# An attention and gated-projection kernel with its whole schedule rewritten, and 65 matmuls on a zero tile added to its opening

## The chip, the cores and the metric

One core of one Trainium2 chip runs the kernel. The metric is the device time of one execution in microseconds (us). The engines are PE (TensorE; PEld is its weight load), DVE (VectorE), ACT (ScalarE), POOL (GpSimd) and SP (SyncE, which here only issues transfers).

## The reference

The first part is causal attention over 4 batches, 8 heads, 768 positions and head size 64. Heads 0, 2 and 6 see all earlier positions, the others only 4 sink positions and a window of 64. The second part is a gated projection of the result.

```python
scores = scale * np.matmul(q, k.transpose(0, 1, 3, 2))
mask = np.where(retr[0, :, 0, 0, None, None], full_mask, stream_mask)
scores = np.where(mask[None, :, :, :], scores, -1000000000.0)
scores = scores - np.max(scores, axis=-1, keepdims=True)
a = np.exp(scores)
a = a / (np.sum(a, axis=-1, keepdims=True) + 1e-09)
attn = np.matmul(a, v)                    # (4, 8, 768, 64)
x = attn.transpose(0, 2, 1, 3).reshape(3072, 512)
h = x @ w_in                              # w_in: (512, 2048)
g = h * (1.0 / (1.0 + np.exp(-beta * h)))
out = g @ w_out                           # w_out: (2048, 512)
```

## The kernel before

The work is cut into 8 chunks (a batch and a half of its 768 positions, 384 rows each) and every chunk into 4 units (a pair of heads), 32 units in all. For a unit, keys and queries are cast to bf16 (`cast`, L246) and turned by PE (`transpose_qk`, L322; from chunk 3 on by transfers), copied to SBUF (`copy_qk`, L330 and L333), multiplied into scores (`steps_QK`, L451), put through the exponential on ACT (L460) and multiplied with the values (`steps_PV`, L520). A column of ones in the value tile gives the sum of a row, by which `normalize` (L529, L533) divides. A pair of units is turned into `xT` (`steps_X` L558 and `copy_x` L567, or by a transfer).

A chunk's rows then go through the first projection in 16 groups (`steps_G1`, L588, then tanh on ACT L593 and the gate on DVE L596) and through the second in blocks of four groups of weights (`steps_G2`, L641). Group i of the first projection needs block i//4 of `w_in`, and step i of the second needs block i of `w_out`; POOL loads these blocks (`load_w_in` L140, `load_w_out` L144). The second projection of chunk 0 is allowed when all its 16 groups are done.

For the first 8 units the masks are added on PE, as a matmul of a mask tile with the identity (`begin`, L422); later units multiply by masks on DVE. At the start, `idle(8, ...)` lets PE do eight matmuls on a tile of zeros (L167). Keys and queries of chunks 0 to 2 are loaded by SP (`load_qk`, L119) and values too (`load_v`, L132); with the letter `g` a load waits for a small fill of its tile on POOL (L115, L129).

The order on every engine is written out by hand. `RAMP` is a list of words that `do` carries out one after the other; each engine keeps the order in which the words give it work. A word has an operation, a unit or chunk, a part, and the engine (v: DVE, a: ACT, g: POOL):
- `ck`, `cq`: cast of keys or queries; `tk`, `tq`: their transposes; `kk`, `kq`: the copies out of PSUM; `ko`: copies for the sink positions
- `ad`: mask matmuls; `qk`: scores; `ex`: exponential; `ma`: a mask on DVE
- `cv`: cast of values; `vo`: sink values; `on`: fills with ones; `pv`: two of a unit's six value products; `no`: normalize
- `xx`, `cx`: transposes and copy to `xT`; `ne`: mask tiles; `be`: the gate's factors
- `lv`, `lq`: loads by SP; `wi`, `wo`: loads of weights by POOL; `ro`: row loads by POOL for chunk 3 and later (L282); `rq`, `rk`: their tiles
- `mm`, `mA`: one group of the first projection (for `mA` in a buffer of the scores); `mb`: one step of the second (four matmuls); `hm`, `hf`: the two halves of one group; `tt`: all transposes and copies of a unit.

`PLAN` has one line for each later unit: `V` scores, `p` a value product, `T` transposes, `X` transposes to `xT`, `a`, `A` and `b` projections, beside words as above. Score tiles have two buffers (`ps_s`), `ps_o` one, and the tiles named `mm` three.

Of the kernel before, what the change touches and what calls it, by code (L numbers as in the profile page):

```python
# [10 lines left out]
F32 = mybir.dt.float32  # L11
# [7 lines left out]
def kernel(  # L19
# [13 lines left out]
    nc = tc.nc  # L33
    B, H, S, D = q.shape
# [5 lines left out]
    HT = HALF // 128  # L40
# [20 lines left out]
    ps_o = ctx.enter_context(tc.tile_pool(name="ps_o", bufs=1, space=bass.MemoryType.PSUM))  # L61
# [94 lines left out]
    zeros = consts.tile([128, 512], BF16, name="zeros")  # L156
# [160 lines left out]
    def transpose_qk(u, name):  # L317

        s = st_u.setdefault(u, {})
        tp = ps_m.tile([128, 512], F32, name="mm").bitcast(BF16)[:, 0:HALF].rearrange("p (t j) -> p t j", t=HT)  # L320
        for t in range(HT):
            nc.tensor.transpose(tp[:, t, :], s["qkb"][:, "qk".index(name), t].rearrange("p h d -> p (h d)"), ident)  # L322
        s["t" + name] = tp
# [58 lines left out]
    def steps_QK(u):  # L382
# [117 lines left out]
        some = 3 if len(tiles) == 3 else 2  # L500
        return [visit(range(i, min(i + some, len(tiles)))) for i in range(0, len(tiles), some)]

    def steps_PV(u):
        b, h2, p = units[u]
        s = st_u.setdefault(u, {})

        def head(hh, qi, last):
            def go():
                for f in s["masks"] + chunk_values[u // NPAIR] if u >= 8 else []:
                    f()  # L510
                if "po" not in s:
                    if u < 8 and u % 2:
                        po = ps_m.tile([128, 512], F32, name="mm")
                        s["po"] = po[:, 0:HT * 2 * (D + 1)].rearrange("p (t h d) -> p t h d", t=HT, h=2)
                    else:
                        s["po"] = ps_o.tile([128, HT, 2, D + 1], F32, name="po")
                po = s["po"]
                lst = s["blocks"][hh][qi]
                for j, (e, val) in enumerate(lst):
                    nc.tensor.matmul(po[:, qi, hh, :], e, val, start=(j == 0), stop=(j == len(lst) - 1))  # L520
                if last and u >= 8:
                    normalize(u)
            return (len(s["blocks"][hh][qi]) * 38, go)
        return [head(hh, qi, hh == 1 and qi == HT - 1) for qi in range(HT) for hh in range(2)]
# [138 lines left out]
    h = FO // 2  # L663
# [21 lines left out]
    def do(word):  # L685

        what, n, i, eng = re.fullmatch(r"([a-z]{2}|[a-z][A-Z])(\d*)\.?(\d*)([vag]?)", word).groups()
        n, i = int(n or 0), int(i or 0)
        if what in ("ck", "cq"):
            cast(n, what[1], copies[eng])  # L690
        elif what in ("tk", "tq"):
            step((170, lambda: transpose_qk(n, what[1])))
        elif what in ("kk", "kq"):
            copy_qk(n, what[1], copies[eng])
        elif what == "ko":
            sinks_of(n)
        elif what in ("ad", "qk", "ex", "ma"):
            if n not in visits:
                visits[n] = steps_QK(n)
            step((0 if what in ("ex", "ma") else 170, lambda: visits[n][what](i)))  # L700
        elif what == "cv":
            cast_v(n, i, copies[eng])
        elif what == "vo":
            sink_values(n)
        elif what == "pv":
            pv = products.setdefault(n, [])
            if not pv:
                pv.extend(steps_PV(n))
            run(pv[:2])
            del pv[:2]  # L710
        elif what == "no":
            normalize(n)
        elif what == "xd":
            x_by_dma(n)
        elif what == "xx":
            run(steps_X(n))
        elif what == "cx":
            copy_x(n, copies[eng])
        elif what == "on":
            ones_v(engines[eng], n)  # L720
        elif what == "ne":
            negatives([(0, 1, 2), (3, 4)][n])
        elif what == "be":
            step((100, beta_go))
        elif what == "lv":
            load_v(n, held=eng == "g", tiles=[i])
        elif what == "lq":
            load_qk(n, i, held=eng == "g")
        elif what == "wi":
            load_w_in(n)  # L730
        elif what == "wo":
            load_w_out(n)
        elif what == "rq":
            rows_queries()
        elif what == "rk":
            rows_keys()
        elif what == "ro":
            if n not in more_rows:
                more_rows[n] = load_rows(n)
            more_rows[n].pop(0)()  # L740
        elif what in ("dk", "dq"):
            transposes_dma(n, what[1])
        elif what == "ml":
            late[n].pop(0)()
        elif what == "tt":
            run(steps_T(n))
        elif what == "hm":
            opened.append(done[0])
            done[0] += 1
            step(halves[0](opened[-1], 0))  # L750
        elif what == "hf":
            step(halves[0](opened.pop(0), 1))
        else:
            feed({"mm": "a", "mA": "A", "mb": "b"}[what])

    def feed(x):
# [34 lines left out]
    PLAN = """
        ro3 ro3 ck9v b cq9a dk3 b cv2.1v cv2.0v vo2 T ro3 cv2.2v V cq11v a ro3 ro3 ro3 ck11a ro4 a b
        ck10a a dq3 a p cq10v a V p T p p p V p
        b T b p p p p p V p
        A b A a V ro4 p V a p p ro4 p p p
        ro4 V b p p p b p p ro4 p V b
        b p p p p X V p p a ro4 a ro4
        b A ro4 a a p V p ro4 p p ro4 b ro4 a a A ro4 A b b b dk4 A V a p dq4 p b A b
        p p p p p V p a a
        p p A p V p p p  # L800
        a a b b p p p p p p V a A A
        a b p p p p V p p
        b b a V p p p p p b a p
        b A A a a A p a A A a p b a p A p p p A A V b b b A
        p V p p p p p
        a A a b b p p p V p p b p a A
        a p A b p b p b A p b a p b p V A a
        V a p p b p p b V p p A
        b p p p p V p p
        A a b V b b a a p p b p A p a p a a A A p b V a b A b b  # L810
        p p p p V p p
        a A V b p A A p p p V p p a A
        a p b V b p p p p p
        V b a p a p p V A p A b b p p A A a
        p b V a p p p p A a p
        b a A p a p a a b a A p p A b a p b a p
        b A X a A b A
    """.strip().split("\n")
# [41 lines left out]
    i = 0  # L860
# [39 lines left out]
```

## Time and profile before

| | |
|---|---|
| median of 3 runs | 228.62 us (228.47 to 229.1) |
| the profiled execution | 231.07 us |
| its span, first to last instruction | 229.1 us |
| PE busy | 223.1 us, 1907 matmuls |
| ACT, DVE, POOL busy | 154.3, 141.8, 87.6 us |
| first projection starts | 24.41 us |
| second projection starts | 48.65 us |

A row of the timeline gives the start, the time from first start to last end, the engine, the line, the operation, the tiles (out<-in), the shape and the count, and in brackets the idle time before it and what ended that. A row of a stretch gives its length, then the busy time and the number of instructions of PE, PEld, DVE, ACT and POOL (of PE alone where only PE was asked for), the clock that the throttle granted, the mean share of the DMA engines (over 1 where packets overlap) and GB/s. A row of waits gives the engine, tile and line that waited, what it waited for, the sum in us, how often, and the longest. Matmuls of one row overlap, so a row is as long as the steps between them and one's own duration.

### The profile page before, as it was taken

How to read it: one execution, taken by the hardware profiler on the slowest of the kernel's cores; microseconds unless marked ns; L12 is line 12 of the kernel's file. 1: busy time of each engine (PE TensorE's matmuls, PEld its weight loads, DVE VectorE, ACT ScalarE, POOL GpSimd, SP SyncE). 2: the span in 40 equal slices, each digit the busy share in tenths (PEclk: the TensorE clock that was granted, in tenths of full speed). 3: DMA queues.
4: the chain of work that ended last, by engine and by line, in shares of the span. 5: the costliest groups of instructions: out<-in, count | busy, mean ns of one | idle time of the engine just before them, and what ended most of it. 6: DMA issues, size and time to landing. Idle time of an engine off the chain costs nothing.

```text
span 229.1 us, 5018 instructions
## 1 busy us (share of the span) xinstructions
PE 223.1 (97%) x1907; PEld 127.4 (56%) x1907; DVE 141.8 (62%) x342; ACT 154.3 (67%) x254; POOL 87.6 (38%) x143
## 2 busy tenths in 40 slices
PE   7899999999999999999999999999999999999994
PEld 2456666654565665555654565455654656455553
DVE  4458988875286588536952588546963779028600
ACT  2567988864868799438944697759876878138621
POOL 5373991219636269535028038940560000000000
PEclk9999999999999999999999999999999999999999
DMA  6999999999999999969778969496983130111012
GB/s 202 262 297 247 215 197 203 232 193 161 196 142 97 181 164 156 122 173 156 111 149 109 158 132 173 86 163 93 194 70 83 47 83 0 49 46 46 0 49 92
DMA packets 95383, 31.66 MB, mean 138 GB/s; under 512 B 81776, under 2 KB 92416, under 8 KB 95360
## 3 DMA queue, kind: packets, MB, share of 16 engines
q1 hardware_dynamic: 58880, 22.82, 48.6%
q0 software_dynamic: 35904, 8.13, 39.8%
q10 hardware_dynamic: 576, 0.40, 0.5%
q8 instruction: 15, 0.25, 0.4%
q14 instruction: 8, 0.07, 0.1%
HBM read 27.27 MB, written 6.29 MB: 146 GB/s over the span
## 4 chain that ended last, share of the span: by engine, by line
PE 94%; DMA 2%; ACT 1%; SPq 0%; issue 0%; ACTq 0%
PE mm L641 35%; PE mm L588 25%; PE sp L588 12%; PE sp L451 8%; PE po L520 7%; PE mm L322 2%; DMA s<-in_k_dram 2%; PE sp L422 2%; PE mm L626 2%; PE mm L558 1%; PE mm L520 1%; PE mm L451 1%; ACT qkb L246 1%; SPq L119 0%; ACT es L460 0%; ACT KT L330 0%
## 5 line engine op out<-in xcount | busy, mean ns | idle before, releaser
L641 PE MATMUL mm<-w_out_sb,gT 128*128 128x512 bf16 x368 | 85.9, 379 | 0.0
L460 ACT ACTIVATE es<-sp 128x768 bf16<-128x768 f32 (+2 forms) x72 | 56.6, 837 | 21.4 <-PE sp L451 21.2
L588 PE MATMUL mm<-xT,w_in_sb 128*128 128x384 bf16 x348 | 64.6, 326 | 0.0
L588 PEld LDWEIGHTS <-w_in_sb 128*128 128x128 bf16 x512 | 47.8, 98 | 29.8 <-issue 0.2
L593 ACT ACTIVATE th<-mm,beta_h 128x384 f32<-128x384 f32 x87 | 49.7, 587 | 5.7 <-PE mm L588 0.9
L641 PEld LDWEIGHTS <-gT 128*128 128x128 bf16 x368 | 33.4, 98 | 36.0 <-issue 1.5
L596 DVE SCALAR_TENSOR_TENSOR gT<-th,mm 128x384 bf16<-128x384 f32 x87 | 46.7, 551 | 6.7 <-ACT th L593 3.2
L282 POOL DMA_DIRECT2D s<-in_q_dram x30 | 22.4, 763 | 26.3 <-DMA QTD<-s 19.8
L588 PE MATMUL sp<-xT,w_in_sb 128*128 128x384 bf16 x164 | 32.3, 326 | 0.0
L645 ACT ACTIVATE osb<-mm 128x512 f32<-128x512 f32 x23 | 13.9, 603 | 25.5 <-PE mm L641 25.2
L520 PEld LDWEIGHTS <-es 128*128 128x128 bf16 x472 | 23.8, 99 | 12.8 <-issue 1.5
L596 DVE SCALAR_TENSOR_TENSOR gT<-th,sp 128x384 bf16<-128x384 f32 x41 | 22.3, 552 | 5.6 <-ACT th L593 3.7
L282 POOL DMA_DIRECT2D s<-in_k_dram x30 | 22.4, 760 | 8.5 <-DMA w_out_sb<-in_moe_w_out_dram 5.8
L593 ACT ACTIVATE th<-sp,beta_h 128x384 f32<-128x384 f32 x41 | 23.7, 585 | 2.3 <-PE sp L588 0.2
L520 PE MATMUL po<-VX,es 128*128 128x65 bf16 x360 | 25.2, 195 | 0.0
L251 POOL CAST VX<-vs 128x512 bf16<-128x512 f32 x16 | 10.1, 632 | 36.4 <-DMA vs<-in_v_dram 30.2
L529 DVE RECIPROCAL rec<-po 128x6 f32<-128x6 f32 x28 | 5.4, 193 | 29.1 <-PE po L520 29.1
L451 PE MATMUL sp<-QTD,KT 64*128 64x128 bf16 (+2 forms) x258 | 20.1, 249 | 0.6 <-ACT QTD L333 0.4
L478 DVE TENSOR_TENSOR es<-es,Mh 128x768 bf16<-128x768 bf16 (+1 forms) x26 | 15.5, 626 | 5.0 <-ACT es L460 4.4
L533 DVE TENSOR_TENSOR x<-po,rec 128x384 bf16<-128x384 f32 x28 | 15.6, 557 | 1.0
L451 PEld LDWEIGHTS <-KT 64*128 64x128 bf16 x278 | 11.4, 96 | 6.2 <-issue 3.9
L259 POOL COPY VO<-VX 128x512 bf16<-128x512 bf16 x16 | 10.8, 696 | 6.2 <-DVE VX L251 6.2
(72 smaller groups left out, 160.3 us busy)
## 6 DMA issues: line engine op xcount, KB each, us to landing
vs<-in_v_dram SPq DMA_DIRECT2D x24, 256.0 KB, 5.2
out_dram<-osb SPq DMA_DIRECT2D x23, 256.0 KB, 2.6
w_in_sb<-in_moe_w_in_dram POOLq DMA_DIRECT2D x4, 512.0 KB, 9.3
w_out_sb<-in_moe_w_out_dram POOLq DMA_DIRECT2D x4, 512.0 KB, 16.8
s<-in_k_dram POOLq DMA_DIRECT2D x30, 64.0 KB, 4.8
s<-in_q_dram POOLq DMA_DIRECT2D x30, 64.0 KB, 4.9
s<-in_k_dram SPq DMA_DIRECT2D x4, 384.0 KB, 6.8
s<-in_q_dram SPq DMA_DIRECT2D x4, 384.0 KB, 6.5
```

Of the source, the lines that this page charges most:

```text
L259: copy(out=vo[:, i - 1, :, 0:D], in_=vx[:, i, :, 0:D])
L282: nc.gpsimd.dma_start(out=ROWS[c % 2, name][:, t, i * 4 * D:(i + 1) * 4 * D].rearrange("p (h d) -> p h d", d=D), in_=src[b, i:H:2, r:r + 1 ...
L451: nc.tensor.matmul(sps[i][r][:, x * 128:y * 128], key(a, lhs), s["QT"][half(a), qi * 128:(qi + y - x) * 128], start=first, stop=first or y ...
L460: nc.scalar.activation(out=views[i].rearrange("p r k j -> p r (k j)"), in_=banks[2][:, :, 0:n * 128], func=ACTF.Exp, scale=scale)
L478: nc.vector.tensor_mul(ev[:, :, 0:n], ev[:, :, 0:n], Mh[h2][:, None, m0:m0 + n].to_broadcast([128, 2, n, 128]))
L520: nc.tensor.matmul(po[:, qi, hh, :], e, val, start=(j == 0), stop=(j == len(lst) - 1))
L533: nc.vector.tensor_mul(xg[g][:, :, :, u % 2, :].rearrange("p a t d -> p t a d"), po[:, :, :, 0:D], rec.to_broadcast([128, HT, 2, D]))
L588: nc.tensor.matmul(hp[:, 0:HALF], w_in_sb[:, mo, fi * 128:(fi + 1) * 128], xT[c][:, mo, :], start=(mo == 0), stop=(mo == MO - 1))
L593: nc.scalar.activation(out=th, in_=hp[:, 0:HALF], func=ACTF.Tanh, scale=beta_h[:, fi:fi + 1])
L596: nc.vector.scalar_tensor_tensor(out=gTs[c][:, fi, :], in0=th, scalar=1.0, in1=hp[:, 0:HALF], op0=ALU.add, op1=ALU.mult)
L641: nc.tensor.matmul(op, gTs[c][:, fi, ns * 128:(ns + 1) * 128], w_out_sb[:, fi, :], start=(fi == 0), stop=(fi == FO - 1))
L645: nc.scalar.activation(out=osb, in_=op, func=ACTF.Copy, scale=0.5)
```

## The change

Both lists are rewritten. The same operations stand in them in another order, some on another engine: for instance the casts `ck3`, `cq3`, `ck6`, `cq6` and `cq7` go to ACT, and `cv0.2` goes from ACT to DVE. The halves `hm` and `hf` become an ordinary group. `tt8` stands in front of all five `mb` of the opening instead of after two; of the six `ro3` in the opening one now stands in front of `wo3`.

A new word, `zz`, calls `keep_busy`: n matmuls of the zero tile with itself, each 122 columns wide, into the columns of the PSUM tile of unit 0's value product that the product does not use. Nobody reads them. The tile of the value product gets the full width of 512 columns for that. There are six lots of ten and one of five: in front of `tq0`, `tq1`, `ad0.0`, `ad0.1`, `ad1.0`, `qk1.0` and the second `pv0`.

```diff
+    banks_o = {}
+
+    def sums_bank(u):
+        if u not in banks_o:
+            banks_o[u] = ps_o.tile([128, 512], F32, name="po")
+        return banks_o[u]
+
+    def keep_busy(n):
+        z = HT * 2 * (D + 1)
+        for i in range(n):
+            nc.tensor.matmul(sums_bank(0)[:, z:512], zeros[:, 0:128], zeros[:, 0:512 - z], start=True, stop=True)
...
-                        s["po"] = ps_o.tile([128, HT, 2, D + 1], F32, name="po")
+                        s["po"] = sums_bank(u)[:, 0:HT * 2 * (D + 1)].rearrange("p (t h d) -> p t h d", t=HT, h=2)
...
     RAMP = """
-        ck0g ne1 lv0.0 lv0.1 tk0 ck2a ne0 cq0v ck1a tq0 kq0a ad0.0 on0v lv0.2 kk0v cq1v tq1 qk0.0
-        tk2 ad0.1 kq1v tk1 kk1v lq1.0g be qk0.1 ex0.0 ad1.0 cv0.0g ko1 lq1.1 ex0.1 pv0 ck3v cq3g tk3
-        lv1.0g cq2a tq2 kk3v lv1.1 cv0.1g ad1.1 qk1.1 kk2v ex1.1 tq3 ko2 qk1.0 wi0 vo0 cq4g lv1.2 cv0.2a
-        lq2.0g ko3 pv0 kq2v pv0 ad2.0 qk2.0 lv2.0 ex1.0 pv1 kq3a pv1 ck4v ad2.1 qk2.1 lv2.1 pv1 ex2.0
...
-        kk6a ml0 tk5 cq7g kq5v ex4.1 kk5a ko5 ko6 ad5.1 tq6 wi1 qk5.0 ex4.0 tk7 tq7 ex5.0 no3
...
-        pv7 pv7 no7 wo3 pv6 no6 rk cq8g xx2 ro3 cx2a mA mA ck8g xx3 cx3a mm mA
...
-        mA mm ro3 mA mm ro3 mm mm ro3 mA mA mb mb tt8 mb mb mb
+        ne1 ck1a on0g lv0.0g ck0g cq0v zz10 tq0 ck2a ne0 cq1v kq0a zz10 tq1 tk0 kk0v zz10 ad0.0 tk2 lv0.1 qk0.0 tk1
+        cq2v zz10 ad0.1 lv0.2 lq1.0g kk1v ck3a ex0.0 kq1a kk2v be qk0.1 zz10 ad1.0 ad1.1 ko1 tk3 lq1.1 cv0.0g tq2
+        ex0.1 cq3a lv1.0g ko2 tq3 pv0 lv1.1 kk3a ko3 wi0 qk1.1 cv0.1v zz10 qk1.0 kq2a vo0 ex1.1 ad2.0 kq3v qk2.0
+        cv0.2v lv1.2 zz5 pv0 ck4v pv0 lq2.0g ex2.0 ad2.1 qk2.1 no0 pv2 cq4g ex1.0 cq5g pv1 pv1 tk4 lv2.0 ad3.0 pv1 no1
+        qk3.0 ad3.1 qk3.1 ex2.1 pv2 tq4 ck6a xx0 kk4v pv2 ex3.0 tk6 kq4v ad4.0 cx0v pv3 ck7g ad4.1 pv3 ad5.0 tq5 ml0
+        on1g qk4.1 ex3.1 cq6a no2 kk6a ck5g pv3 cq7a lv2.1 qk4.0 tk5 tq6 ad5.1 ex4.1 kq5v kk5a ko5 ko6 qk5.0 tk7 tq7
+        lv2.2 no3 qk5.1 ex4.0 wi1 ex5.0 wi2 ex5.1 lq2.1 kq6v kq7v xx1 ad6.0 ml1 ml1 qk6.0 ma5.0 ad6.1 qk6.1 cx1a wi3
...
+        ex7.0 qk7.1 ex7.1 pv5 pv5 rk wo1 pv5 mm wo2 pv6 lv3.1 pv7 cq8g pv6 no5 pv6 pv7 ro3 pv7 no6 no7 wo3 xx2 cx2a
...
+        mm mA mm mA mm mA mb mb mb mb mb
     """
...
     PLAN = """
-        ro3 ro3 ck9v b cq9a dk3 b cv2.1v cv2.0v vo2 T ro3 cv2.2v V cq11v a ro3 ro3 ro3 ck11a ro4 a b
...
+        ck9v dk3 ro3 cq9v A ro3 cv2.0v T cv2.1v vo2 ro3 ro3 cv2.2v V ro3 a b ro3 cq11v
...
```

More of the change, by code (lines that the diff above doesn't have):

```diff
@@ L746, in do @@
             run(steps_T(n))
+        elif what == "zz":
+            keep_busy(n)
         elif what == "hm":
@@ L771 @@
     RAMP = """
-        ck0g ne1 lv0.0 lv0.1 tk0 ck2a ne0 cq0v ck1a tq0 kq0a ad0.0 on0v lv0.2 kk0v cq1v tq1 qk0.0
-        tk2 ad0.1 kq1v tk1 kk1v lq1.0g be qk0.1 ex0.0 ad1.0 cv0.0g ko1 lq1.1 ex0.1 pv0 ck3v cq3g tk3
-        lv1.0g cq2a tq2 kk3v lv1.1 cv0.1g ad1.1 qk1.1 kk2v ex1.1 tq3 ko2 qk1.0 wi0 vo0 cq4g lv1.2 cv0.2a
-        lq2.0g ko3 pv0 kq2v pv0 ad2.0 qk2.0 lv2.0 ex1.0 pv1 kq3a pv1 ck4v ad2.1 qk2.1 lv2.1 pv1 ex2.0
-        ad3.0 tq4 no0 tk4 ex2.1 ck7g kk4a qk3.0 ad3.1 qk3.1 no1 pv2 ck6v ex3.0 cq5v ck5g pv2 tk6
@@ L777 @@
-        xx0 ad4.0 cq6g pv3 kq4v ex3.1 pv2 ad4.1 cx0v ad5.0 qk4.1 pv3 lv2.2 no2 on1g tq5 pv3 qk4.0
-        kk6a ml0 tk5 cq7g kq5v ex4.1 kk5a ko5 ko6 ad5.1 tq6 wi1 qk5.0 ex4.0 tk7 tq7 ex5.0 no3
-        qk5.1 ex5.1 kq6v xx1 ad6.0 kk7v wi2 kq7v wi3 cx1a qk6.0 ml1 ad6.1 ex6.0 cv1.1g ko7 qk6.1 cv1.0v
-        ex6.1 hm lq2.1 ma5.0 ma5.1 mm cv1.2g vo1 mm wo0 pv4 lv3.0g ad7.0 lv3.1 pv4 hf pv4 no4
-        qk7.0 ad7.1 pv5 pv5 ex7.0 lv3.2 qk7.1 pv5 no5 ml1 wo1 ex7.1 pv6 pv6 wo2 mm pv7 rq
-        pv7 pv7 no7 wo3 pv6 no6 rk cq8g xx2 ro3 cx2a mA mA ck8g xx3 cx3a mm mA
@@ L783 @@
-        mm mA mm mm mA mm mm mm mA mm ro3 mm mm mA mm mm mm ro3
-        mA mm ro3 mA mm ro3 mm mm ro3 mA mA mb mb tt8 mb mb mb
+        ne1 ck1a on0g lv0.0g ck0g cq0v zz10 tq0 ck2a ne0 cq1v kq0a zz10 tq1 tk0 kk0v zz10 ad0.0 tk2 lv0.1 qk0.0 tk1
+        cq2v zz10 ad0.1 lv0.2 lq1.0g kk1v ck3a ex0.0 kq1a kk2v be qk0.1 zz10 ad1.0 ad1.1 ko1 tk3 lq1.1 cv0.0g tq2
+        ex0.1 cq3a lv1.0g ko2 tq3 pv0 lv1.1 kk3a ko3 wi0 qk1.1 cv0.1v zz10 qk1.0 kq2a vo0 ex1.1 ad2.0 kq3v qk2.0
+        cv0.2v lv1.2 zz5 pv0 ck4v pv0 lq2.0g ex2.0 ad2.1 qk2.1 no0 pv2 cq4g ex1.0 cq5g pv1 pv1 tk4 lv2.0 ad3.0 pv1 no1
@@ new lines @@
+        qk3.0 ad3.1 qk3.1 ex2.1 pv2 tq4 ck6a xx0 kk4v pv2 ex3.0 tk6 kq4v ad4.0 cx0v pv3 ck7g ad4.1 pv3 ad5.0 tq5 ml0
+        on1g qk4.1 ex3.1 cq6a no2 kk6a ck5g pv3 cq7a lv2.1 qk4.0 tk5 tq6 ad5.1 ex4.1 kq5v kk5a ko5 ko6 qk5.0 tk7 tq7
+        lv2.2 no3 qk5.1 ex4.0 wi1 ex5.0 wi2 ex5.1 lq2.1 kq6v kq7v xx1 ad6.0 ml1 ml1 qk6.0 ma5.0 ad6.1 qk6.1 cx1a wi3
+        ex6.0 ex6.1 ma5.1 cv1.1g kk7v mm cv1.0g ko7 mm cv1.2g vo1 lv3.0g rq ad7.0 mm pv4 pv4 pv4 ad7.1 qk7.0 wo0 no4
+        ex7.0 qk7.1 ex7.1 pv5 pv5 rk wo1 pv5 mm wo2 pv6 lv3.1 pv7 cq8g pv6 no5 pv6 pv7 ro3 pv7 no6 no7 wo3 xx2 cx2a
@@ L785 @@
+        lv3.2 mA mA mm ro3 xx3 cx3v mm mA mm ck8a mm mA mA mm ro3 ro3 mm mA mm mm mm mA mm mm mA mm tt8 ro3 mA mm ro3
+        mm mA mm mA mm mA mb mb mb mb mb
     """
@@ L791 @@
     PLAN = """
-        ro3 ro3 ck9v b cq9a dk3 b cv2.1v cv2.0v vo2 T ro3 cv2.2v V cq11v a ro3 ro3 ro3 ck11a ro4 a b
[L793 to L817, printed above, removed]
+        ck9v dk3 ro3 cq9v A ro3 cv2.0v T cv2.1v vo2 ro3 ro3 cv2.2v V ro3 a b ro3 cq11v
+        b b A dq3 A ro4 p p V ck11a p ck10a p p p b cq10v V b T
+        b T b p V p p p p p b a
+        a p p V p p V A p p
+        V a b p p V p p p p ro4 A
+        ro4 ro4 b X p V b p p b A p p p a ro4 b
+        ro4 a p V ro4 p p p a a ro4 ro4 b A ro4 A dk4 b a ro4 ro4 a p A V dq4 a p a b
+        p p p A p V p p
+        A b A p p p p p p A V
+        A a p p b p p V p a a p a
+        b p p V p p p p
+        b a a p V p p p p p a
+        a A A b b p a A A a p a a p b A p p b a V p A a A a
+        p V p a A p p p p
+        b A A a b p p p b p a a p p b V b a A
+        A p a a A a A a p V p p p p a a
+        p V p a b V p p p p A b
+        p p a p p V p p
+        b V b p b p a p V b p A p p b a A b A a A a
+        b b A p p b p p p a V p A b a
+        p V a A p p p A p V p b A
+        p p V p p p p
+        b V A a a V A p b p b a A A p p b a p p a
+        A b b p b V a p a A b p A p A p b a p a A
+        p p p p p p
+        A a X a A A A b b
     """.strip().split("\n")
```

## The prediction

> **What bounds the kernel now.** I read the page first, then PE's waits, then PE's busy time by stretch.
>
> ```profile
> PE 223.1 (97%) x1907; PEld 127.4 (56%) x1907; DVE 141.8 (62%) x342; ACT 154.3 (67%) x254; POOL 87.6 (38%) x143
> ...
> PEclk9999999999999999999999999999999999999999
> DMA  6999999999999999969778969496983130111012
> ...
> PE 94%; DMA 2%; ACT 1%; SPq 0%; issue 0%; ACTq 0%
> ```
> ```profile
> PE mm L167 <- DVE zeros L157: 1.3, 1, 1.3
> PE mm L322 <- DVE qkb L246: 0.7, 2, 0.5
> PE sp L451 <- ACT QTD L333: 0.4, 1, 0.4
> ```
> ```profile
> 24.40:225.00 200.60, 200.60 (x1699) 115.06 (x1696) 126.52 (x303) 139.43 (x229) 74.55 (x105) 1.00 0.89 125
> ```
> PE is 94% of the chain. From 24.4 us, where the first projection begins, it is busy in all 200.60 us of 200.60 (the second column), so the new order can gain nothing there; it can only open a gap. Whatever is won must be won before 24.4 us, and it stays won only if nothing later, above all a transfer, holds PE up. The DMA row is at 9 from the second slice to the seventeenth (5.7 to 97 us): transfers have no reserve in that time.
>
> In the ramp PE waits little (1.1 us besides the start), but it is slow. The PEclk row does not show that; the durations of equal rows on PE's timeline do:
>
> ```profile
> 1.29 3.59 PE L167 MATMUL mm<-zeros 128*128 128x512 bf16 x8 [1.29 <-DVE zeros L157]
> 4.83 0.50 PE L322 MATMUL mm<-idb,qkb 128*128 128x128 bf16 x3
> 5.51 0.50 PE L322 MATMUL mm<-idb,qkb 128*128 128x128 bf16 x3 [0.17 <-DVE qkb L246]
> ...
> 12.47 0.50 PE L322 MATMUL mm<-idb,qkb 128*128 128x128 bf16 x3
> ...
> 17.10 0.66 PE L322 MATMUL mm<-idb,qkb 128*128 128x128 bf16 x6
> ...
> 18.70 0.33 PE L322 MATMUL mm<-idb,qkb 128*128 128x128 bf16 x3
> ...
> 34.35 1.46 PE L588 MATMUL mm<-xT,w_in_sb 128*128 128x384 bf16 x8
> ```
> ```profile
> L167 PE MATMUL mm<-zeros 128*128 128x512 bf16 x8 | 3.6, 628 | 1.3 <-DVE zeros L157 1.3
> ...
> L588 PE MATMUL mm<-xT,w_in_sb 128*128 128x384 bf16 x348 | 64.6, 326 | 0.0
> ```
> Three transposes take 0.50 us at 4.83 and at 12.47, but 0.33 at 18.70. So PE runs slow until about 17.4 us, inside the row at 17.10 (six in 0.66). Matmuls of a row overlap, so their step is what is left of the row without one's own duration (the groups' means above): the zero matmuls step by (3.59 - 0.63)/7 = 0.42 us for 512 columns, 0.83 ns a column; the projections by (1.46 - 0.33)/7 = 0.16 us for 384, 0.42 ns a column. The ramp runs at half speed.
>
> **What brings full speed.** The ramp's slow part with all engines, and two stretches of it, PE alone:
>
> ```profile
> 4.83:17.43 12.60, 11.39 (x94) 6.43 (x94) 6.93 (x20) 7.12 (x12) 6.64 (x20) 1.00 1.18 281
> ```
> ```profile
> 10.61:14.02 3.41, 3.29 (x33) 1.00 1.08 315
> 14.02:17.43 3.41, 3.41 (x33) 1.00 1.21 273
> ```
> The switch came after a stretch without a gap that began between 10.61 and 14.02, so after 3.4 to 6.8 us. The unbroken stretch from 1.29 to 5.33 (the 0.17 us gap before 5.51) brought none, so 4.0 us were not enough there. In the new order the first ten zero matmuls stand behind the eight that exist, the first transposes have their data by then, and ten more follow; PE has no gap from 1.29 to about 7 us. I estimate the switch 4.0 to 6.8 us after 1.29, at 5.3 to 8.1, and take 6.5.
>
> [...]
>
> **The price of the zero matmuls.** Each has 512 - 390 = 122 columns: 0.10 us slow, 0.051 us fast. A lot of ten costs 1.0 or 0.51. The first lot and most of the second run slow (1.0 + 0.75), the other 45 fast (2.3): about 4.1 us of PE in all. PE's own work from 4.83 to 20.9 us (the transposes ahead of the key copy `kk5a`) halves in its slow part: the 11.39 us busy of the row above would be about 5.7, and 3.5 (17.4 to 20.9) follow. From 4.7, the end of the eight: 4.7 + 5.7 + 3.5 + 4.1 = 18.0, against 20.9 now. So PE stops setting the pace if another engine needs longer than 18.0; ScalarE does.
>
> **ScalarE's chain, the term of the gain.** The waits of all engines from 4 to 25 us, and rows of ACT's timeline:
>
> ```profile
> ACT es L460 <- PE sp L451: 4.1, 6, 1.4
> ...
> ACT KT L330 <- PE mm L322: 0.9, 2, 0.6
> ```
> ```profile
> 6.29 0.93 ACT L246 CAST qkb<-s 128x384 bf16<-128x384 f32 x2 [2.92 <-DMA s<-in_k_dram]
> 7.12 0.47 ACT L333 COPY QTD<-mm 128x384 bf16<-128x384 bf16 x1
> 8.18 0.81 ACT L460 ACTIVATE es<-sp 128x768 bf16<-128x768 f32 x1 [0.59 <-PE sp L451]
> ...
> 13.07 0.61 ACT L251 CAST VX<-vs 128x512 bf16<-128x512 f32 x1
> ...
> 21.29 0.48 ACT L330 COPY KT<-mm 128x384 bf16<-128x384 bf16 x1 [0.25 <-PE mm L322]
> ...
> 23.53 0.83 ACT L567 COPY xT<-mm 128x768 bf16<-128x768 bf16 x1
> ```
> The first projection (24.41, below) starts when `cx1a` (23.53 + 0.83) ends, and that stands behind `kk5a` (21.29) on ACT. ACT loses 4.1 + 0.9 = 5.0 us in that time to a late PE. Of these the new order keeps some:
> - The first exponential needs `kk0v`, whose transposes now stand behind two lots and `tq0`, `tq1`: 4.7 + 1.0 + 0.3 + 0.75 + 0.35 = 7.1, a copy of 0.5 (as at 7.12) and latencies to 7.85, `qk0.0` to about 8.25, the exponential at 8.45, 0.3 later than 8.18. With `ck3a` in front of it ACT waits 0.5 there.
> - The second one waits 0.3 (`kq1a` fills the rest).
> - The score tiles have two buffers, and `ad2.0` now follows `ex1.1` at once. In the chain of waits
>
> ```profile
> 14.17 0.43 PE sp L422 x2
> 14.60 0.43 PE sp L451 x2
> ```
>  these two steps took 0.86 slow, so 0.43 fast and some 0.35 of latencies: ACT waits 0.8.
> - The rest 0.3. Together 1.9, so 3.1 are saved.
>
> ACT also takes on work ahead of `kk5a`: 13 casts and copies instead of 9, at 0.46 (half of the 0.93 row), less 0.15 because `cv0.2` (0.61) went to DVE. That is 4 x 0.46 - 0.15 = 1.7, of which `ck1a` now lies in the wait for the first keys (-0.46) and part of `ck3a` before the first exponential (counted above, so nothing more). 1.2 remain. **The ramp ends 3.1 - 1.2 = 1.9 us earlier**; with the switch at 5.3 or 8.1 us instead of 6.5, by 2.6 or 1.4. What hides the zero matmuls from then on is ACT: without that cover each lot would cost its 0.51.
>
> Cost at nothing: `lv0.0g` now waits on POOL's fill behind `on0g`, and SP's loads stand behind it; up to 0.5 us, covered by a DMA queue already full. DVE and POOL were busy 6.93 and 6.64 of 12.60 us, so the few casts that change places between them have room. The rewritten PLAN holds the same matmuls in another order; from 24.4 us I put it at nothing, and the last rival at a loss.
>
> **What takes part of it back: the last block of the second weights.** The work on POOL and on PE around it:
>
> ```profile
> 21.83 0.53 POOL L312 COPY KO<-KT 128x128 bf16<-128x128 bf16 x2 [3.82 <-ACT KT L330]
> 22.30 2.22 POOL L140 DMA_DIRECT2D w_in_sb<-in_moe_w_in_dram  x3
> ```
> ```profile
> 24.41 1.80 PE L588 MATMUL mm<-xT,w_in_sb 128*128 128x384 bf16 x10
> ...
> 48.65 1.89 PE L641 MATMUL mm<-w_out_sb,gT 128*128 128x512 bf16 x8
> ...
> 50.71 4.48 PE L641 MATMUL mm<-w_out_sb,gT 128*128 128x512 bf16 x20
> ```
> ```profile
> L144 POOL DMA_DIRECT2D w_out_sb<-in_moe_w_out_dram x4: 745/755/770, 27.7 to 30.0; - x4
> ...
> DMA to landing us min/median/max: 11.9/16.8/21.2
> ```
> ```profile
> s<-in_k_dram POOLq DMA_DIRECT2D x2, 64.0 KB, 21.3
> ```
> ```profile
> L282 POOL DMA_DIRECT2D s<-in_k_dram x5: 740/745/775, 31.1 to 40.0; - x5
> ...
> DMA to landing us min/median/max: 17.5/20.5/21.6
> ```
> The last two fences are the `ro3` loads: the first two of them alone, then five with their first and last start. The fourth block lands at 30.0 + 21.2 = 51.2. Its first user, the fourth `b` step, starts at 50.71 + 0.86 = 51.57 (a step is four matmuls of 512 columns at 0.42 ns): 0.4 us to spare. In the new order that step comes 1.9 us earlier. POOL issues `wi1` behind `ko5`, `ko6`, which wait for `kk5a` (3.82 us now), so the queue of weights also starts 1.9 us earlier. But one `ro3` is now in front of `wo3`. The first of these lands at 31.1 + 21.3 and the fifth at 40.0 + 17.5, so they are (57.5 - 52.4)/4 = 1.25 us apart. By bytes it would be 0.5: 64 KB against a block's 512 (128 x 4 x 512 values of two bytes), and blocks land (51.2 - 39.6)/3 = 3.9 apart, the first at 27.7 + 11.9. I take 1.25, the same transfer on the same queue. The block then lands 1.25 - 0.4 = 0.85 late (0.1 by bytes), PE waits for it once, and being full afterwards never makes it up. `tt8`, now ahead of the `b` steps, was ahead of the fourth one before, so it costs nothing.
>
> **Sum:** -1.9 + 0.85 = -1.05 us. The profiled execution's own 231.07 (span 229.1) would become 230.0; it ran 2.45 above the median of the runs, 228.62, which becomes 227.57, say **227.5**.
>
> **Rivals.**
> - *Nothing given back* (0.20): the `ro3` costs 0.5 and hides in the spare 0.4. Gain 1.8 to 2.6: 226.0 to 226.8, about 226.7. For it speaks the size by bytes.
> - *The weights do not come earlier* (0.17, slower): the DMA row has no reserve, so the fourth block, with an `ro3` ahead, lands at 51.2 + 1.25 = 52.45 whatever POOL does; its step then starts 0.85 later than now: 229.5. It decides from the point at which the queue of weights moves by less than 0.85. Against it: the transfers of SP that share the engines (chunk 2's keys and queries) are not needed until later and can give way.
> - *The zeros do not bring the clock* (0.08): then all 65 run slow, 6.6 us, of which PE's idle 1.2 us takes a part: up to 5.4 us, at most 234.0. For it: the eight zeros at the start brought nothing.
> - *The gain is lost elsewhere in the new order* (0.11): a value cast or transfer of the second chunk comes last instead, 228.6 give or take 0.6.
>
> [...]
>
> **How the numbers follow.** The forecast has 0.44, its own range 226.9 to 228.1. A measurement of this kernel tells about 0.3% (0.69 us) from no change. Faster by more: 0.36 of the forecast, 0.20 of the first rival, 0.01: 0.57. Within: 0.08 + 0.03 + 0.07 = 0.18. Slower: 0.14 + 0.08 + 0.03 = 0.25. The range 226.0 to 229.6 takes in the first two rivals and leaves out the slow clock.
>
> **What would show it.** Right: transposes of three take 0.33 us from about 7 us on; `cx1a` ends near 22.4 and the first projection follows; one PE wait of about 0.9 us on the w_out block near 50 us; PE full from then on. Wrong: slow rows beyond 8.1 us, ACT still waiting over 3 us for scores, more than one gap of PE after 24 us, or a first projection no earlier than 23.5.

## The result and the profile after

The changed kernel takes 231.03 us (median of 22 runs, 229.59 to 234.53), the kernel before 229.51 (22 runs, 228.21 to 233.02): a ratio of 1.0066, 95% interval 1.0037 to 1.0095. It is slower by 0.7%, where 227.5 us and faster had been forecast. Every ratio here leaves out, on both sides, runs more than 1.5% above the fastest run of their kernel, so where many are left out (six runs of a2 and five of d1, in the table below) it is smaller than the medians beside it would give.

The two profiled executions say the opposite: spans of 228.8 and 229.1 us. That contradiction is the subject of what follows. Below are lines of the page after, then PE's waits, PE's timeline and ACT's timeline of the changed kernel. Its line numbers are 13 higher from L500 on: L533 is the value product, L601 the first projection and L654 the second; L514 are the new zero matmuls.

```profile
PE 220.8 (97%) x1953; PEld 129.8 (57%) x1972; DVE 138.1 (60%) x340; ACT 154.9 (68%) x257; POOL 85.4 (37%) x143
...
PE 78%; DMA 12%; POOL 4%; ACT 2%; issue 1%; DVE 1%; ACTq 0%; SPq 0%
```
```profile
PE mm L654 <- DMA w_out_sb<-in_moe_w_out_dram: 0.8, 1, 0.8
PE sp L451 <- ACT KT L330: 0.4, 1, 0.4
PE sp L422 <- ACT es L460: 0.4, 2, 0.2
```
```profile
4.68 1.23 PE L514 MATMUL po<-zeros 128*128 128x122 bf16 x10
5.70 0.44 PE L322 MATMUL mm<-idb,qkb 128*128 128x128 bf16 x3
5.97 0.70 PE L514 MATMUL po<-zeros 128*128 128x122 bf16 x10
...
7.49 0.33 PE L322 MATMUL mm<-idb,qkb 128*128 128x128 bf16 x3
...
23.09 1.47 PE L601 MATMUL mm<-xT,w_in_sb 128*128 128x384 bf16 x8
...
50.89 2.75 PE L654 MATMUL mm<-w_out_sb,gT 128*128 128x512 bf16 x12 [0.81 <-DMA w_out_sb<-in_moe_w_out_dram]
```
```profile
16.45 0.51 ACT L246 CAST qkb<-s 128x384 bf16<-128x384 f32 x1 [0.92 <-DMA s<-in_k_dram]
...
19.96 0.48 ACT L330 COPY KT<-mm 128x384 bf16<-128x384 bf16 x1
...
22.20 0.83 ACT L580 COPY xT<-mm 128x768 bf16<-128x768 bf16 x1
```
Ten zeros take 1.23 us at 4.68 and 0.70 at 5.97: full speed came between, as forecast. The first projection starts at 23.09 instead of 24.41, the wait for the fourth block of `w_out` is 0.81 us. In this pair of traces the forecast's steps appear, with the first projection 0.6 us later than the sum has it. So either the trace of before was no usual one, or the time is lost in executions that this pair does not show.

### The profile page after: what moved, and what is told of

It reads as the page before. It is cut to its first block, busy times and chain, and to the rows that moved or that the text cites. A ratio compares the mean times of both kernels' runs of the same rounds, so it can differ in the third digit from the quotient of the medians.

```text
span 228.8 us, 5128 instructions
## 1 busy us (share of the span) xinstructions
PE 220.8 (97%) x1953; PEld 129.8 (57%) x1972; DVE 138.1 (60%) x340; ACT 154.9 (68%) x257; POOL 85.4 (37%) x143
## 3 DMA queue, kind: packets, MB, share of 16 engines
q1 hardware_dynamic: 58880, 22.82, 50.9%
## 4 chain that ended last, share of the span: by engine, by line
PE 78%; DMA 12%; POOL 4%; ACT 2%; issue 1%; DVE 1%; ACTq 0%; SPq 0%
PE mm L654 33%; PE mm L601 19%; DMA w_out_sb<-in_moe_w_out_dram 9%; PE sp L601 9%; PE po L533 6%; PE sp L451 6%; DMA s<-in_k_dram 3%; PE mm L167 2%; PE mm L639 2%; POOL w_in_sb L140 1%; PE po L514 1%; PE mm L322 1%; ACT es L460 1%; POOL VX L251 1%; POOL w_out_sb L144 1%
## 5 line engine op out<-in xcount | busy, mean ns | idle before, releaser
L654 PE MATMUL mm<-w_out_sb,gT 128*128 128x512 bf16 x349 | 84.3, 379 | 1.8 <-DMA w_out_sb<-in_moe_w_out_dram 0.8
L601 PEld LDWEIGHTS <-w_in_sb 128*128 128x128 bf16 x512 | 48.0, 98 | 30.7
L601 PE MATMUL mm<-xT,w_in_sb 128*128 128x384 bf16 x344 | 64.1, 326 | 0.0
L606 ACT ACTIVATE th<-mm,beta_h 128x384 f32<-128x384 f32 x86 | 48.9, 589 | 6.9 <-PE mm L601 3.4
L654 PEld LDWEIGHTS <-gT 128*128 128x128 bf16 x368 | 33.1, 98 | 35.0 <-issue 2.2
L658 ACT ACTIVATE osb<-mm 128x512 f32<-128x512 f32 x23 | 13.8, 600 | 28.3 <-PE mm L654 27.7
L601 PE MATMUL sp<-xT,w_in_sb 128*128 128x384 bf16 x168 | 32.7, 326 | 0.0
L533 PEld LDWEIGHTS <-es 128*128 128x128 bf16 x472 | 23.4, 98 | 12.8 <-issue 1.0
L606 ACT ACTIVATE th<-sp,beta_h 128x384 f32<-128x384 f32 x42 | 24.3, 586 | 5.2 <-PE sp L601 3.0
L609 DVE SCALAR_TENSOR_TENSOR gT<-th,sp 128x384 bf16<-128x384 f32 x42 | 23.0, 553 | 5.7 <-ACT th L606 3.7
L533 PE MATMUL po<-VX,es 128*128 128x65 bf16 x360 | 25.3, 194 | 0.1
L451 PE MATMUL sp<-QTD,KT 64*128 64x128 bf16 (+2 forms) x258 | 19.1, 240 | 0.6 <-ACT KT L330 0.4
L478 DVE TENSOR_TENSOR es<-es,Mh 128x768 bf16<-128x768 bf16 (+1 forms) x26 | 13.3, 543 | 6.9 <-ACT es L460 6.3
L546 DVE TENSOR_TENSOR x<-po,rec 128x384 bf16<-128x384 f32 x28 | 15.6, 557 | 1.0
L259 POOL COPY VO<-VX 128x512 bf16<-128x512 bf16 x16 | 9.8, 636 | 10.1 <-DVE VX L251 10.1
```

The costliest lines, as they stand in the source:

```text
L451: nc.tensor.matmul(sps[i][r][:, x * 128:y * 128], key(a, lhs), s["QT"][half(a), qi * 128:(qi + y - x) * 128], start=first, stop=first or y ...
L478: nc.vector.tensor_mul(ev[:, :, 0:n], ev[:, :, 0:n], Mh[h2][:, None, m0:m0 + n].to_broadcast([128, 2, n, 128]))
L546: nc.vector.tensor_mul(xg[g][:, :, :, u % 2, :].rearrange("p a t d -> p t a d"), po[:, :, :, 0:D], rec.to_broadcast([128, HT, 2, D]))
L601: nc.tensor.matmul(hp[:, 0:HALF], w_in_sb[:, mo, fi * 128:(fi + 1) * 128], xT[c][:, mo, :], start=(mo == 0), stop=(mo == MO - 1))
L606: nc.scalar.activation(out=th, in_=hp[:, 0:HALF], func=ACTF.Tanh, scale=beta_h[:, fi:fi + 1])
L609: nc.vector.scalar_tensor_tensor(out=gTs[c][:, fi, :], in0=th, scalar=1.0, in1=hp[:, 0:HALF], op0=ALU.add, op1=ALU.mult)
```

## The experiments

Each kernel was timed beside the kernel before; "first" is the start of the first projection in its one trace. "Lost" counts the runs in which PE had the full clock and lost it for 3.4 us or more, told by the mean granted clock of the run: 3.4 us of it give a mean of 0.993 (the traces of a5 and b2), 6.8 give 0.983 (b4), and a trace without one has 0.996 or more. A run counts from 0.993 down. Of all 138 timed runs of the kernel before, 71 count.

| kernel | median (range), us | ratio, 95% interval | lost | first, us | span, us |
|---|---|---|---|---|---|
| the change | 231.03 (229.59 to 234.53) | 1.0066, 1.0037 to 1.0095 | 0 of 22 | 23.09 | 228.8 |
| a1, before again | 230.56 (228.27 to 233.72) | 1.0007, 0.996 to 1.0054 | 6 of 12 | 21.70 | 226.6 |
| a2, change, no zeros | 232.64 (229.3 to 234.44) | 1.0088, 1.0043 to 1.0133 | 8 of 12 | 22.15 | 227.3 |
| a3, new RAMP, old PLAN | 230.79 (229.15 to 234.27) | 1.0049, 1.001 to 1.0088 | 1 of 12 | 23.08 | 227.8 |
| a5, old RAMP, new PLAN | 230.6 (228.24 to 231.59) | 1.0029, 0.9989 to 1.0069 | 8 of 12 | 23.04 | 228.3 |
| a4, old order, 65 zeros | 229.69 (229.2 to 230.8) | 1.0004, 0.9975 to 1.0033 | 0 of 12 | 23.04 | 227.7 |
| a6, change, `wo3` first | 230.87 (229.6 to 232.29) | 1.0058, 1.0022 to 1.0093 | 0 of 12 | 22.84 | 227.5 |
| a7, old order, 14 zeros | 228.71 (228.21 to 231.22) | 0.9975, 0.994 to 1.0009 | 1 of 12 | 21.82 | 226.6 |
| a8, before, no zeros at all | 230.91 (229.87 to 232.25) | 1.0044, 1.0008 to 1.008 | 0 of 12 | 22.73 | 228.6 |
| c1, change, weights early | 230.03 (229.61 to 231.01) | 1.0023, 0.9992 to 1.0054 | 0 of 12 | 23.11 | 227.8 |
| c5, change, 14 zeros | 230.7 (229.66 to 237.23) | 1.005, 1.001 to 1.009 | 1 of 12 | 22.23 | 227.7 |
| c4, a7 again | 228.74 (228.01 to 229.51) | 0.9973, 0.9942 to 1.0003 | 0 of 12 | 21.68 | 226.2 |
| c3, a7 and `wi1` early | 228.71 (228.01 to 233.24) | 0.996, 0.992 to 0.9999 | 1 of 12 | 21.85 | 226.3 |
| d2, c3 again | 229.04 (227.83 to 230.54) | 0.9963, 0.9937 to 0.999 | 1 of 12 | 22.20 | 226.9 |
| d1, c1 and c5 together | 234.98 (230.81 to 240.41) | 1.012, 1.0072 to 1.0169 | 8 of 10 | 21.98 | 235.6 |

**Was the trace of before a usual one?** a1 is the kernel before, unchanged.

> The kernel before, unchanged, for a second trace. Theory A (the first trace of before was an unlucky one: its clock came up at 17.4 us, other executions get it earlier and so have little to win from the zero matmuls): the ratio is 1.00 within 0.3%, the three-transpose rows turn from 0.50 to 0.33 us before 15 us in this trace, and the first projection starts before 24.0 us. Theory B (every execution of before switches at about 17.4 us, and the new order loses 1.5 us somewhere that its trace did not show): ratio 1.00, switch between 16 and 19 us, first projection at 24.4.

PE's timeline in a1:

```profile
4.83 0.50 PE L322 MATMUL mm<-idb,qkb 128*128 128x128 bf16 x3
5.51 0.50 PE L322 MATMUL mm<-idb,qkb 128*128 128x128 bf16 x3 [0.17 <-DVE qkb L246]
...
6.71 0.34 PE L322 MATMUL mm<-idb,qkb 128*128 128x128 bf16 x3 [0.50 <-DVE qkb L246]
...
21.70 1.80 PE L588 MATMUL mm<-xT,w_in_sb 128*128 128x384 bf16 x10
```
Full speed came at about 6 us instead of 17.4, and the first projection at 21.70 instead of 24.41. The span is 2.5 us shorter. Theory A stands: the first trace showed one of the longer executions. The 138 timed runs say how usual it is. The 71 that lost the clock had it before. Of the other 67, 27 take at most 228.82 us and 40 take 229.2 to 232.3; the first trace, at 231.07 with a mean of 1.000, is of this last kind. A third trace, b4,

> A third trace of the kernel before. Theory A: its switch to full speed lies somewhere between 4.5 and 17.5 us and the start of the first projection follows it (21.5 us for a switch at 6, 24.4 for 17.4), and from there on the spans differ by no more than 0.6 us from that difference.

shows a third way. PE alone, by stretch:

```profile
4.80:8.20 3.40, 2.08 (x24) 0.99 1.11 300
8.20:11.60 3.40, 3.05 (x25) 0.50 1.21 240
11.60:14.90 3.30, 3.30 (x35) 0.50 1.08 325
15.00:18.00 3.00, 3.00 (x51) 1.00 1.25 243
```
Three transposes take 0.34 us at 4.83 in b4, so full speed was there by 4.8 us. The clock (third number from the end) was lost at about 8.1 and came back after 14.9. The first projection starts at 22.95, the span is 227.6 us. a5 has the same RAMP and the new PLAN:

```diff
     PLAN = """
-        ro3 ro3 ck9v b cq9a dk3 b cv2.1v ...
+        ck9v dk3 ro3 cq9v A ro3 cv2.0v ...
```


> The RAMP of before, without zeros, with the new PLAN. If the loss sits in the ramp: ratio 0.998 to 1.002. If it sits in the new PLAN: ratio 1.004 to 1.015, with waits of PE after 55 us that before does not have.

```profile
4.80:8.20 3.40, 1.20 (x14) 1.00 1.15 302
8.20:11.60 3.40, 3.40 (x26) 0.50 1.15 231
11.60:15.00 3.40, 2.88 (x41) 0.99 1.10 333
```
Here the clock was lost for 3.4 us only. With the old RAMP the clock therefore goes three ways or more, and the first projection starts between 21.7 and 24.4 us. a5's time does not settle what the new PLAN costs: its interval holds both expectations' values. a3 is the reverse, the new RAMP with the PLAN of before:

> The new RAMP with its zeros, with the PLAN of before. If the loss sits in the ramp (zeros, or the late fourth block of w_out behind a row load): ratio 1.004 to 1.010, and PE's wait for w_out near 50 us is in the trace. If it sits in the new PLAN: ratio 0.993 to 1.000.

Its ratio says that the ramp loses, although the expected wait for `w_out` was not in its trace.

**What are the zeros worth?** a8 takes away the eight zeros that were there:

```diff
-    idle(8, ps_m, "mm")
```


> The kernel before without the eight zero matmuls at its start. Theory A: full speed then always comes late (0.50 us rows until at least 11 us in the trace), ratio 1.006 to 1.015, no run under 229.5 us. If full speed always came late in before (the forecast's view): ratio 0.999 to 1.002.

```profile
10.86 0.97 PE L321 MATMUL mm<-idb,qkb 128*128 128x128 bf16 x6
...
12.20 0.34 PE L321 MATMUL mm<-idb,qkb 128*128 128x128 bf16 x3
```
Full speed comes near 11.5 us and no run is under 229.87: the old zeros do buy an early clock, in some executions. The ratio, 1.0044, is less than the expected 1.006. a2 takes the 65 out of the new order, a4 puts them into the old one:

```diff
-        ne1 ck1a on0g lv0.0g ck0g cq0v zz10 tq0 ck2a ne0 cq1v kq0a zz10 tq1 ...
+        ne1 ck1a on0g lv0.0g ck0g cq0v tq0 ck2a ne0 cq1v kq0a tq1 ...
```


> The new order without the 65 zero matmuls. Theory A: the zeros win nothing on the median, because the clock comes up early enough without them, and the loss is in the order: ratio to before 1.003 to 1.010, like the change itself. Theory C (the zeros themselves cost, 65 x 0.05 us = 3.4 us of PE, partly covered): ratio 0.99 to 1.000. The forecast's mechanism (the zeros are worth 1.9 us to this order): ratio 1.012 to 1.020.

```diff
-        ck0g ne1 ... ck1a tq0 kq0a ad0.0 on0v lv0.2 kk0v cq1v tq1 qk0.0
+        ck0g ne1 ... ck1a zz10 tq0 kq0a zz10 ad0.0 on0v lv0.2 kk0v cq1v zz10 tq1 qk0.0
```


> The order of before, with the same seven lots (65 zero matmuls) in front of the same words. Theory A (the moment at which full speed comes differs from execution to execution; where it comes early by itself the zeros only cost, some 0.9 us, where it comes late they save up to 2.5): ratio 0.998 to 1.006. The forecast's view (full speed is always late without the zeros): ratio 0.985 to 0.995. Theory D (the order alone is at fault, zeros are free): ratio 0.990 to 1.000.

First projections of a2 and of a4:

```profile
22.15 1.47 PE L601 MATMUL mm<-xT,w_in_sb 128*128 128x384 bf16 x8
```
```profile
23.04 1.80 PE L601 MATMUL mm<-xT,w_in_sb 128*128 128x384 bf16 x10
```
Among traces with an early clock, the zeros delay it by 23.09 - 22.15 = 0.94 us in the new order and by 23.04 - 21.70 = 1.34 in the old. They are not hidden by ScalarE. What they buy is that the clock mostly stays: no run of the change, none of a4 and one of 12 of a3 lost it, against 8 of 12 in a2 and about half of before. a4's twelve runs lie within 1.6 us (a1's within 5.5), and its median equals that of before. a2 did not decide between its theories: 1.0088 is in the range of theory A, but the interval reaches the 1.012 of the forecast's mechanism, and half of its runs are left out of it. Its own trace, with full speed by 6.0 us (six transposes in 0.51), is fast. Against a1 the new order costs 22.15 - 21.70 = 0.45 us there. That is not clear of the spread between traces: with an early clock that stays and at most 14 zeros, the first projection starts at 21.68 to 22.20 us in the five traces of the old order and at 21.98 to 22.23 in the three of the new. With 65 zeros it starts at 22.84 to 23.73 in all eight, so the delay by the zeros is clear.

**Few zeros.** a7, and c4 again, put 14 where the old order waits:

```diff
-        ... ck1a tq0 kq0a ad0.0 on0v lv0.2 kk0v cq1v tq1 qk0.0
+        ... ck1a zz2 tq0 kq0a ad0.0 on0v lv0.2 kk0v cq1v zz4 tq1 zz4 qk0.0
...
+        ... ex0.1 zz4 pv0 ...
```


> The order of before with 14 zero matmuls only (2 before tq0, 4 each before tq1, qk0.0 and the first pv0), about as many as its own gaps hold at half speed. Theory A: they cost at most 0.3 us and bring full speed before 9 us more often: ratio 0.993 to 0.999 and fewer runs over 231 us. If zeros do not matter, or the number of 14 is too small to change the activity: 0.999 to 1.001.

> The order of before with 14 zeros once more. Theory A: ratio 0.994 to 0.999 again; if the first sample was chance: 0.999 to 1.002.

First projections at 21.82 and 21.68 us, as early as in a1, and no run of c4 over 229.51. Both intervals just reach past 1. c5 does the same to the new order:

> The changed kernel with 14 zeros (2 before tq0, 6 before tq1, 2 each before ad0.0, ad0.1 and ad1.0) instead of 65. If the 51 others cost their time on the way (0.9 us between the traces with and without them): ratio 1.000 to 1.004, first projection near 22.1 us instead of 22.9. If they are covered by ScalarE: 1.005 to 1.008, first projection at 22.8 to 23.1.

The first projection is at 22.23, so the 51 other zeros did cost 0.86 us, as the first theory had it. But the time hardly moved (1.005, at the edge of the second theory's range): something else dominates there.

**The weights.** a6 puts `wo3` back in front of the row load:

```diff
-        ... cq8g pv6 no5 pv6 pv7 ro3 pv7 no6 no7 wo3 xx2 cx2a
+        ... cq8g pv6 no5 pv6 pv7 wo3 pv7 no6 no7 ro3 xx2 cx2a
```


> The changed kernel with wo3 issued before the ro3 that stood in front of it; nothing else differs. If that row load makes the fourth block of w_out late: wo2 and wo3 land 3.3 to 3.6 us apart instead of 5.4, PE's wait of 0.8 us for w_out is gone, ratio to before 1.000 to 1.006. If the block is late for another reason (the engines that move data are full): still a wait over 0.4 us, ratio 1.004 to 1.010.

PE's waits in a6 name no `w_out` any more:

```profile
PE mm L167 <- DVE zeros L157: 1.3, 1, 1.3
PE mm L322 <- DVE qkb L246: 0.5, 1, 0.5
PE sp L451 <- ACT KT L330: 0.4, 1, 0.4
PE sp L422 <- ACT es L460: 0.2, 1, 0.2
```
The wait is explained by the row load: the third and fourth block land 3.4 us apart (27.7 + 17.1 = 44.8 and 32.6 + 15.6 = 48.2, issue and time to landing), in the first trace of the change 5.4 (28.0 + 17.5 = 45.5 and 29.9 + 21.0 = 50.9). But the time barely changed: five of its runs lie at 229.6 to 229.9 and six at 231.2 to 232.3. Three more traces of the change, b1 to b3, look for the upper group.

> The changed kernel once more, for its trace: where do its executions of 231 to 233 us lose what its first trace (230.9) did not? Theory E: full speed comes by 7.2 us in every execution (lots of zeros fill every stretch from 1.29 to 7), the first projection starts between 22.5 and 24.0 us, and the rest of the spread comes from transfers: PE's wait for w_out near 50 us is between 0.5 and 2.5 us and grows with the span. Theory F: in some executions full speed comes late or is lost again (rows of 0.50 us after 8 us), and the first projection starts after 24 us.

For b2 and b3 the same was expected in short, with a wait for `w_in` before 35 us added to theory E. b1 (230.60 us) and b3 (230.29) look like the first trace, though b3 has no wait for `w_out`. b2 (234.23) does not. Its waits, PE's timeline, and PE by stretch:

```profile
PE sp L601 <- DMA w_in_sb<-in_moe_w_in_dram: 1.9, 1, 1.9
```
```profile
31.12 1.96 PE L601 MATMUL sp<-xT,w_in_sb 128*128 128x384 bf16 x8 [1.94 <-DMA w_in_sb<-in_moe_w_in_dram]
```
```profile
28.00:31.00 3.00, 1.18 (x29) 1.00 1.18 201
...
32.00:35.00 3.00, 3.00 (x15) 0.50 1.21 196
```
The second block of `w_in` is late, PE waits 1.9 us, and from 32.0 to 35.4 us its clock is at 0.50; half of those 3.4 us, 1.7, is what that costs by estimate. Theory E was half right: full speed came early and a transfer made PE wait, but the wait is only 1.9 of the 3.4 us by which the span exceeds the first trace's, and F's lost clock followed. The timed runs of the change differ from b2 in this: none of the 22 lost the clock, and the longest, 234.53 us, has a mean of 1.000. No trace shows one of these. c1 issues that block earlier, and `wo3` as in a6:

```diff
-        on1g qk4.1 ex3.1 cq6a no2 kk6a ck5g pv3 ... lv2.2 no3 qk5.1 ex4.0 wi1 ex5.0
+        on1g qk4.1 ex3.1 cq6a no2 kk6a ck5g wi1 pv3 ... lv2.2 no3 qk5.1 ex4.0 ex5.0
```


> The changed kernel with wi1 issued on POOL right after ck5g, ahead of ko5 and ko6, and wo3 ahead of the ro3. Theory G (the second block of w_in comes last before the fifth group, at random by up to 2.5 us, and makes the upper group of executions): no PE wait for w_in or w_out in the trace, the upper group is gone (spread of the runs under 1.8 us), ratio 0.998 to 1.003. If the upper group has another cause: spread still over 2.5 us and ratio 1.004 to 1.008.

As theory G said: twelve runs within 1.4 us, none over 231.01, ratio 1.0023. a6, with `wo3` moved alone, kept the upper group, so it is the block of `w_in` that makes it. The ratio itself is not clearly better, since its interval overlaps that of the change. What is left is the 1.4 us later first projection (23.11 against 21.70).

c3 and d2 issue `wi1` ahead of `ko5` in the old order with 14 zeros.

> The order of before with 14 zeros, and wi1 issued ahead of ko5. Theory G: if the block of w_in also limits this one, its runs over 229.5 us go and the ratio is 0.993 to 0.997. If the earlier block only takes the transfers' share from the values of chunk 1: 0.999 to 1.004, with waits of POOL or PE for vs near 22 us.

> The order of before with 14 zeros and wi1 ahead of ko5, once more. If the first sample held: ratio 0.993 to 0.998; if it was chance: 0.999 to 1.002.

The ratios are 0.996 and 0.9963, with both intervals below 1: the one version measured faster than before, by 0.4%. The earlier `wi1` is not shown to do any of it, since a7 and c4 without it have 0.9975 and 0.9973. Theory G's sign did not come either: three of c3's runs still lie over 229.5 us. d1 joins c1 and c5.

> The changed kernel with 14 zeros as in c5 and the weight blocks issued early as in c1. If zeros and late blocks are the whole loss beside 0.4 us of order: first projection near 22.2 us, no PE wait for w_in or w_out, runs within 2 us of each other, ratio 0.997 to 1.001. If the order holds another loss: 1.002 to 1.006.

It missed. PE's waits and its stretches:

```profile
PE po L533 <- POOL VX L251: 6.1, 2, 5.7
```
```profile
24.00:28.00 4.00, 0.80 (x10) 1.00 1.20 229
28.00:32.00 4.00, 1.05 (x11) 0.58 1.18 229
```
With 51 zeros fewer, POOL reaches `wi1` earlier still, at 16.29 us instead of 17.65 in c1. The last values of chunk 1 now land 16.5 us after their issue, against 9.2 in c5 and 8.4 in c1. PE waits 6.1 us for the values, and the clock is at 0.58 in the stretch from 28 us. That the earlier block takes the transfers' share from them is argued from this and not shown. What the new order costs without zeros and late blocks was therefore not measured; the 0.45 us from the traces of a2 and a1 is all there is.

## Why the prediction was wrong

- **Full speed at 6.5 us: right.** It came between 5.7 and 6.0 in the first trace of the change.
- **Gain of the ramp in the pair of traces, 1.9 us: 1.32 was measured.** ACT's waits for PE were sized well, at 1.7 us of the 1.9 expected. But ACT also waited 0.92 us for keys (at 16.45, above), a transfer that the sum had left out.
- **Give-back at the fourth block, 0.85 us: right in size (0.81), partly by luck.** The row load put 1.9 us between the third and the fourth block (5.4 apart instead of 3.5), where the sum has 1.25 (its division gives 1.28). And the blocks and the step did not both come 1.9 us earlier: the third block came 2.2 earlier, the step 1.5. a6 shows that the row load does it, but also that it is not what moves the median.
- **Zeros hidden by ScalarE: wrong.** They cost 0.94 and 1.34 us on the way. The lots stand ahead of matmuls whose scores ACT is waiting for, so where the clock is early they delay ACT itself. Its wait for scores from 4 to 25 us is 1.0 us in a2 and 1.5 in the change, and 2.0 in a1 and 3.5 in a4. The lines of a2 and a4 (those of the other two follow below):

```profile
ACT es L460 <- PE sp L451: 1.0, 2, 0.7
...
ACT es L460 <- PE sp L451: 3.5, 4, 1.2
```
- **The step that failed is the sum.** It took -1.05 us from one execution and moved it to the median: 228.62 to 227.57. The profiled 231.07 stood 2 us above all three runs shown, and the text put that down as a constant. It was the late clock, the very thing the change removes. The term that this made too large is the 5.0 us that ACT loses to a late PE. The same waits in a1, and then in the change:

```profile
ACT qkb L246 <- DMA s<-in_k_dram: 2.5, 1, 2.5
ACT es L460 <- PE sp L451: 2.0, 4, 0.9
ACT KT L330 <- PE mm L322: 0.8, 2, 0.5
```
```profile
ACT qkb L246 <- DMA s<-in_k_dram: 3.3, 4, 1.6
ACT es L460 <- PE sp L451: 1.5, 3, 0.8
ACT KT L330 <- PE mm L322: 0.2, 1, 0.2
```

In a1, where the clock comes early by itself, ACT loses 2.8 us instead of 5.0, so only 1.1 is saved and not 3.1. Against that stand the 1.2 us of work that ACT takes on and 0.8 of longer waits for keys. The first projection came 1.39 us later than in a1 (23.09 against 21.70), where 1.9 earlier had been forecast.
- **The moment of full speed.** It varies with the same program: in three traces of before it came by 4.8 us (with a loss at 8.1), at about 6, and at 17.4. The prediction allowed for this in the changed kernel alone.
- **The rivals.** None named the second block of `w_in`, which had 0.4 us to spare as well (in the first trace of before it lands at 29.6 us and is used at 29.95). "The gain is lost elsewhere" came nearest, at 0.11, with too small a price. That the eight zeros at the start brought nothing, as another rival says, holds for the first trace only: without them full speed comes near 11.5 us in a8, and no run of a8 is under 229.87. The statement that nothing after 24.4 us could be won was right; the risk of a loss there was priced at a tenth.

Put together: the spans of the first trace of the change and of a1, both with an early clock that stays, differ by 2.2 us. The first projection makes 1.4 of them and the wait at `w_out` 0.8, which two of the four traces of the change have. In b2 another 3.6 were lost at `w_in`. Against that the change removes late clocks worth up to 2.7 us and the losses of the clock, which before has only in some executions. That the shares add up to the 1.5 us between the medians is argued from these traces, not shown.

## What to carry to other kernels

Before a term is taken from a trace, ask whether that execution stands in the middle of the runs; if it lies 1% above them, look for what made it slow, and take a second trace. Filler work belongs only in gaps, and in no more than they hold: in the old order 14 zeros did nearly what 65 did (3 of 48 runs lost the clock, against none of 12 with 65 and 71 of 138 of before), and the first projection started no later. Where the queue of transfers is full, look at what a load that is moved up may hold back: c1 moved a block up and gained evenness, d1 moved it up further and PE waited 6.1 us for values. In b2 a wait of 1.9 us was followed by 3.4 us at a clock of 0.50.

## What the hardware showed that was not expected

PE's clock, once full, was lost again in some executions: it was at 0.50 from 8.2 to 11.6 us in a5, from 8.1 to 14.9 in b4 and from 32.0 to 35.4 in b2. In the 3.4 us before that PE was busy for 1.20 us in a5, 2.08 in b4 and 1.48 in b2. a2 kept the clock through two stretches as long with hardly more, 2.20 and 2.28. PE by stretch in b2 and in a2:

```profile
28.55:31.97 3.42, 1.48 (x22) 1.00 1.22 202
```
```profile
5.66:9.07 3.41, 2.20 (x28) 1.00 1.23 279
9.07:12.49 3.42, 2.28 (x31) 1.00 1.19 269
```
In b4 the clock did not come back after 8.2 to 11.6 us, with PE busy for 3.05 of 3.40 us, and was back after 3.30 of 3.30 that followed; in a5 it was back after 3.40 of 3.40. Nor did full speed come at one moment after the same start: in c4, as in the first trace of before, PE starts at 1.29 us with the eight zeros, and three transposes at 4.83 take 0.34 us in c4 and 0.50 there.

```profile
1.29 3.22 PE L167 MATMUL mm<-zeros 128*128 128x512 bf16 x8 [1.29 <-DVE zeros L157]
4.83 0.34 PE L322 MATMUL mm<-idb,qkb 128*128 128x128 bf16 x3 [0.31 <-POOL s L115]
```
The landing of the second `w_in` block after its issue varied with the same program between 7.1 (b3) and 9.5 us (b2):

```profile
21.00:22.00 1.00, 0.87 (x14) 0.56 (x14) 0.39 (x2) 1.00 (x3) 0.86 (x3) 1.00 0.25 52
22.00:23.00 1.00, 1.00 (x16) 0.60 (x12) 1.00 (x4) 1.00 (x3) 1.00 (x2) 1.00 0.50 97
```
These rows are of b2. Just when the block was issued there, at 21.6 us, the transfer engines were a quarter to a half busy (second number from the end); b3 has 0.37 and 0.82 in the same stretches. What decides between the two was not settled.
